# Five of nine key tiles of each head enter the value product as a rounded part and a rest

## The chip, the cores and the metric

The kernel runs on one core of a Trainium2 chip. The metric is the device time of one execution, in microseconds (us). The core's engines are named as the profile names them: PE (TensorE, matrix products; PEld is its loading of weights), DVE (VectorE), ACT (ScalarE), POOL (GpSimd) and SP (SyncE, whose queue issues all DMAs of this kernel). Each works through its own instructions in program order and waits for the others by semaphores.

## The reference

Three stages follow one another; all inputs and the output are float32.

```python
# attention: 2 batches x 8 heads, 1152 keys, 576 queries after pooling, width 64
q_pool = q.reshape(B, H, S // 2, 2, D).mean(axis=3)
scores = (1 / sqrt(D)) * (q_pool @ k.T)
attn = exp(scores - max(scores));  attn = attn / (sum(attn) + 1e-9)
x = attn @ v                                  # -> 1152 tokens x 512
# gated layer, 512 -> 1536 -> 512
x = ((x @ w_a) * (x @ w_b)) @ w_out
# four experts, 512 -> 1024 -> 512
p = probs / (probs.sum(-1) + 1e-9)
out = sum over e of p[:, e] * (max(x @ w1[e], 0) @ w2[e])
```

## The kernel before

**Attention.** The 16 heads go one after the other, and two heads (a pair) share their loads and preparations. Keys are cut into nine tiles of 128, queries into two halves of 288 columns (`HQ`). A score step `qk` (line 515) makes four products of a rounded format (fp32r): the high parts of keys and queries (L528, operands `A`, `QH`), then the rests together with the row of subtracted maxima (L533, `B`, `QL`). They fill one of two score buffers `st` in PSUM; ACT takes the exponential of 128x576 scores into a tile `e` in SBUF (L538), from a pool of `NE` = 8. A step `pv` (line 540) multiplies an `e` tile with the value tile `VF` in full float32 (L543): two products of 288 columns, and the profile has two records for each. `VF` holds the 64 value columns of the head, and ones in the other 64, so the same product gives the sum of the exponentials.

**The maxima.** For each pair, 27 max steps (`mx`) make a 128x384 product (L418) into one of two PSUM buffers, and DVE reduces it (L433). PE can thus be two max steps ahead of DVE. After the 27th, DVE folds the maxima into a column tile `mc` (L447), PE turns it by a product (L456), DVE copies the row (L458, `mr`), and a DMA puts it into `QL` of the next head; without it that head's scores can't start.

**Preparations of a pair** are `k` (the rounding of the keys, ACT), `klo0` to `klo2` (the rests of the keys in thirds of 128x384, DVE, L333), `qs`, `qh`, `ql` (the same for the queries) and the puts `da`, `db`, `dh`, `dl` (DMAs that lay them out as the operands of one head), `qb` (the operand `QB` of the max steps) and `row`. The loads are `lq`, `lk0` to `lk2` and `ldf` (values). `evac` copies a finished head out of PSUM (ACT), `nr`, `nb` and `n` divide it by its sums and split the result into `X`, high part and rest (L597, L283, L602).

**The order** of all of it is written out by hand: `FIRST` for heads 0 and 1, `PROG` for the rest, whose first nine lines that begin with `qk` are an even head and whose other nine are an odd one. A word stands for one step; a step goes to each engine's queue at the place where its word stands. In head 0, `A` and `C` are score steps on the first 256 and the last 320 queries, `x` and `y` the max steps of heads 0 and 1, `a` and `c` products with the values. The table `ENG` says which engine does a preparation (V is DVE, P is POOL, A is ACT).

**The later stages** (line 876 on) are products of three rounded terms (`mm3`, L884): high times high, high times rest, rest times high. While attention runs, the words `w` decode the first weights on DVE, ACT and POOL; POOL's only part in it is one subtraction per piece (L188). The first gated columns are started at the end of attention, and their products with the last pair come last.

Of the kernel before, what the change touches and what calls it, by code (L numbers as in the profile page):

```python
# [7 lines left out]
F32 = mybir.dt.float32  # L8
# [10 lines left out]
HQ = SQ // 2  # L19
# [28 lines left out]
C  # L48
C klo0 y a y a y c y c klo2 y y qh
C c y  # L50
# [17 lines left out]
qk n mx dl db mx pv pv da klo0 mx  # L68
qk mx pv
qk mx pv evac mx  # L70
qk lq klo1
qk mx mx pv mx pv ql mx ldf mx pv mx
qk klo2 lk0 mx
qk mx nr pv mx mx nb pv
qk w
qk mx dl lk1 mx pv qs mx dh
qk mx lk2 pv da w mx
qk mx db pv n mx n
qk pv mx evac k mx
qk w qh  # L80
qk qb n pv rm pv ldf
qk pv n pv w
qk
qk w n pv w
# [7 lines left out]
def kernel(  # L92
# [138 lines left out]

    with tc.manual_schedule():
        att = ExitStack()
        kq_p = att.enter_context(tc.tile_pool(name="kq", bufs=2))
        pair_p = att.enter_context(tc.tile_pool(name="pair", bufs=2))
        lo_p = att.enter_context(tc.tile_pool(name="lo", bufs=2))
        b_p = att.enter_context(tc.tile_pool(name="b", bufs=1))
        e_p = att.enter_context(tc.tile_pool(name="e", bufs=NE))
        m_p = att.enter_context(tc.tile_pool(name="m", bufs=2))
        u_p = att.enter_context(tc.tile_pool(name="u", bufs=2))  # L240
        r_p = att.enter_context(tc.tile_pool(name="r", bufs=1))
# [7 lines left out]
        def psum(kind, base, n, count):  # L249
# [5 lines left out]
        At, Bt, QHt, QLt, VFt = (  # L255
            [b_p.tile([128] + shape, dt, name=f"{n}{i}") for i in range(2)]
            for n, shape, dt in (
                ("A", [S], F32R), ("B", [S], F32R), ("QH", [SQ], F32R), ("QL", [SQ], F32R),
                ("VF", [KT, 128], F32),
            )  # L260
        )

# [9 lines left out]

        def fill_v(i, e):
            e.memset(VFt[i][:, :, rows(1 - i)], 1.0)

        engs = {"V": nc.vector, "P": nc.gpsimd, "A": nc.scalar}

# [11 lines left out]
        emitted = set()  # L289
        every = slice(0, 128)  # L290

        q_p = att.enter_context(tc.tile_pool(name="q", bufs=2))
        q_t = {}

        def load_first():
# [224 lines left out]
            if c == 1:  # L520
                den_gather(0, 0, U_t[0][64:65])

        def qk(h, t):
# [13 lines left out]
            e = E_t[h, t] = e_p.tile([128, 2, C1], F32, tag="e", name="e")[:, :, :HQ]  # L537
# [121 lines left out]
        nc.scalar.activation(out=nid, in_=nid_s, func=AF.Copy)  # L659
        own_qh(0, nc.scalar, c1)  # L660
# [8 lines left out]
        emitted |= {("row", 0), ("vf", 0), ("vf", 1)}  # L669
        emitted |= {(x, h) for x in "abhl" for h in range(2)}  # L670
        puts = {x: 2 for x in "abhl"}
        nxt_ld = {"lq": 2, "lk0": 2, "lk1": 2, "lk2": 2, "ldf": 2}
        nxt_pre = {"k": 1, "qs": 1, "qh": 1, "qb": 1}
        emitted |= {(x, 1) for x in ("lq", "lk0", "lk1", "lk2")} | {("ql", 0)}
# [13 lines left out]
        def first(tok):  # L688
# [22 lines left out]
            elif tok == "y":  # L711
                assert n < 5 * KR and {"dh1", "da1"} <= emitted
                max_step(1, n)
            elif tok == "R1":
                assert count["y"] == 5 * KR
                max_col(0, slice(5, 9))
                max_col(0, slice(9, 10), KR, 64)
                row_one()
                emitted.add(("row", 1))
            elif tok in ("E1", "E2"):  # L720
                assert count["ac"[tok == "E2"]] == KT
                evac_half(tok == "E2")
                emitted.add(("evac", 0) if tok == "E2" else "E1")
            else:
                need = {"kl1": "kh1", "ql1": "qh1", "dh1": "qh1", "db1": "kh1", "da1": "kl1"}
                assert tok not in need or need[tok] in emitted
                {
                    "qs1": lambda: own_qs(1, nc.gpsimd),
                    "qh1": lambda: own_qh(1, nc.scalar),
                    "kh1": lambda: own_kh(1, slice(0, S)),  # L730
                    "kl1": lambda: [own_klo(1, r, nc.gpsimd) for r in range(KR)],
                    "ql1": lambda: own_ql(1, nc.gpsimd),
                    "da1": lambda: own_put_kl(1, slice(0, S)),
                    "dh1": lambda: own_put_qh(1),
                    "db1": lambda: put(Bt[1][rows(1), :], At[1][rows(1), :]),
                    "lv1": lambda: [fill_v(1, nc.gpsimd), load_v(1)],
                    "zq": lambda: nc.gpsimd.memset(QB.bitcast(F32), 0.0),
                }[tok]()
                emitted.add(tok)

        for h in range(1, min(NHX, NH)):
# [3 lines left out]
            for tok in FIRST if h == 1 else PROG[half:] if h % 2 else PROG[:half]:  # L745
# [28 lines left out]
                elif tok == "pv":  # L774
# [3 lines left out]
                    assert ("qk", hh, j) in emitted  # L778
                    if j == 0:
                        assert ("vf", hh) in emitted  # L780
                    pv(hh, j)
                    pv_at[0] += 1
                elif tok == "evac":
                    fresh = 1
                    if h > 0:
# [20 lines left out]
                elif tok in ("lq", "lk0", "lk1", "lk2"):  # L806
                    p = nxt_ld[tok]
                    if p < NH // 2:
                        nxt_ld[tok] += 1
                        if tok == "lq":  # L810
                            assert ("qs", p - 1) in emitted
                            load_q(p)
                        else:
                            r = int(tok[2])
                            assert all((f"klo{x}", p - 1) in emitted for x in range(KR if r == 0 else r + 1))
# [46 lines left out]
            return  # L862

        rest = list(range(pv_at[0] - (NH - 1) * KT, KT))
        for j in rest:
            pv(NH - 1, j)
        evac(NH - 1)
# [197 lines left out]
```

## Time and profile before

| what | us |
| --- | --- |
| median of 3 runs | 907.93 (907.48 to 909.01) |
| the profiled execution, own time | 909.75 |
| its span, first to last instruction | 908.0 |
| busy: PE, DVE, ACT, POOL | 893.5, 459.1, 270.8, 72.1 |
| a pair of heads in the steady part (182.60 to 214.48) | 31.88 |
| end of attention, start of the gated layer's unbroken stretch | 282.4, 308.2 |

The granted TensorE clock is 1.00 in every stretch that the profile lists, which is the upper of its two levels, 2.4 GHz. Attention ends at 282.4 us, the other two stages take the rest. A busy time is the time in which an engine had an instruction running; ends of matmuls are modelled, so the spacing of their starts says more than their length. The chain of waits goes back from the last instruction, at each step to what released it.

### The profile page before, as it was taken

The numbers are of one execution on the slowest core, as the hardware profiler recorded it, in microseconds if no ns is written. First come the engines' busy times: TensorE is split into PE (matmuls) and PEld (weight loads), VectorE is DVE, ScalarE is ACT, GpSimd is POOL, SyncE is SP. The second block draws the span as 40 slices with busy tenths as digits, with TensorE's granted clock in tenths as the row PEclk, the third lists the DMA queues.
The fourth block names the chain that finished last, engine by engine and source line by source line (L and its number), as shares of the span: only waits on it lengthen the run. The fifth ranks groups of instructions, "written<-read, shape, count | busy, mean of one in ns | idle before, by whom it ended". The sixth has DMA issues, their size and how long they took to land.

```text
span 908.0 us, 11502 instructions
## 1 busy us (share of the span) xinstructions
PE 893.5 (98%) x4709; PEld 816.6 (90%) x4709; DVE 459.1 (51%) x792; ACT 270.8 (30%) x395; POOL 72.1 (8%) x43
## 2 busy tenths in 40 slices
PE   7999999999999999999999999999999999999998
PEld 5787888888889999999999999889988998899986
DVE  5875757766604888988785243113321242124311
ACT  4344455445453333333321232002300231003200
POOL 7000000000000222222222000000000000000000
PEclk9999999999999999999999999999999999999999
DMA  7557576857450222112222112001300121011011
GB/s 180 125 147 206 144 177 171 190 135 174 108 123 1 93 93 93 75 55 75 99 70 94 43 57 88 1 0 47 132 8 1 47 93 47 1 40 54 4 54 47
DMA packets 49385, 76.99 MB, mean 85 GB/s; under 512 B 32496, under 2 KB 36084, under 8 KB 45748
## 3 DMA queue, kind: packets, MB, share of 16 engines
q1 hardware_dynamic: 49332, 76.25, 29.5%
q8 instruction: 37, 0.61, 0.3%
q14 instruction: 16, 0.13, 0.0%
HBM read 51.96 MB, written 2.39 MB: 60 GB/s over the span
## 4 chain that ended last, share of the span: by engine, by line
PE 91%; DMA 3%; DVE 3%; ACT 1%; SPq 1%; issue 1%; ACTq 0%; DVEq 0%
PE PS L884 44%; PE PS L1007 22%; PE PS L543 12%; PE PS L418 4%; PE PS L528 3%; PE PS L533 3%; PE PS L508 1%; DMA kq<-in_kq_dram 1%; DMA dc<-D 1%; DMA B<-kh 1%; DMA QH<-QH 1%; DMA A<-kh 0%; DVE R L872 0%; SPq L390 0%; DMA rd<-rc 0%
## 5 line engine op out<-in xcount | busy, mean ns | idle before, releaser
L884 PE MATMUL PS<-X,w 128*128 128x384 f32 x2016 | 351.7, 335 | 0.6 <-ACT asb L910 0.5
L884 PEld LDWEIGHTS PS<-X,w 128*128 128x128 f32 x2016 | 349.8, 188 | 1.8 <-ACT asb L910 1.2
L1007 PE MATMUL PS<-w,hs 128*128 128x512 f32 x864 | 197.3, 390 | 0.0
L1007 PEld LDWEIGHTS PS<-w,hs 128*128 128x128 f32 x864 | 162.2, 188 | 33.3
L543 PE MATMUL PS<-e,VF 128*128 128x288 f32 x540 | 149.7, 408 | 0.7 <-ACT U L564 0.3
L433 DVE TENSOR_REDUCE m<-PS 128x1 f32<-128x384 f32 (+1 forms) x213 | 112.1, 554 | 57.9 <-PE PS L418 54.5
L980 ACT ACTIVATE hs<-PS 128x1152 fp32r<-128x1152 f32 x32 | 36.3, 1134 | 281.3 <-PE PS L884 281.3
L538 ACT ACTIVATE e<-PS 128x576 f32<-128x576 f32 x135 | 84.4, 648 | 108.0 <-PE PS L533 107.2
L543 PEld LDWEIGHTS PS<-e,VF 128*128 128x128 f32 x540 | 98.4, 190 | 20.0 <-ACT U L564 0.9
L981 DVE SCALAR_TENSOR_TENSOR hs<-PS,hs 128x1152 fp32r<-128x1152 f32 x32 | 43.5, 1358 | 134.3 <-ACT hs L980 134.3
L188 POOL TENSOR_TENSOR t<-v,w 128x512 f32<-128x512 f32 (+2 forms) x22 | 56.1, 2550 | 409.1 <-ACT w L178 367.9
L1016 DVE SCALAR_TENSOR_TENSOR acc<-PS,p_n,acc 128x512 f32<-128x512 f32 x27 | 20.3, 751 | 115.7 <-PE PS L1007 115.7
L884 PE MATMUL PS<-G,w 128*128 128x384 f32 x432 | 75.0, 334 | 0.0
L884 PEld LDWEIGHTS PS<-G,w 128*128 128x128 f32 x432 | 74.9, 188 | 0.0
L418 PE MATMUL PS<-kh,QB 128*128 128x384 f32 x189 | 72.7, 425 | 1.5 <-DVE m L433 1.1
L528 PE MATMUL PS<-QH,A 128*128 128x288 f32 x270 | 65.1, 322 | 2.6 <-ACT e L538 2.6
L533 PE MATMUL PS<-QL,B 128*128 128x288 f32 x270 | 57.4, 294 | 0.0
L528 PEld LDWEIGHTS PS<-QH,A 128*128 128x128 f32 x270 | 47.9, 189 | 9.0 <-ACT e L538 3.7
L418 PEld LDWEIGHTS PS<-kh,QB 128*128 128x128 f32 x189 | 34.9, 189 | 10.0 <-DVE m L433 4.2
L533 PEld LDWEIGHTS PS<-QL,B 128*128 128x128 f32 x270 | 43.3, 188 | 0.0
L223 DVE TENSOR_TENSOR w<-stg,w 128x1024 fp32r<-128x1024 f32 x32 | 38.9, 1215 | 8.1 <-ACT w L222 8.1
L193 DVE TENSOR_TENSOR w<-t,c 128x512 fp32r<-128x512 f32 (+2 forms) x44 | 39.2, 931 | 1.0
(84 smaller groups left out, 480.5 us busy)
## 6 DMA issues: line engine op xcount, KB each, us to landing
stg<-in_w_dram SPq DMA_DIRECT2D x16, 1024.0 KB
stg<-in_wab_dram SPq DMA_DIRECT2D x12, 1024.0 KB
stg<-in_wout_dram SPq DMA_DIRECT2D x8, 768.0 KB
VF<-in_vo_dram SPq DMA_DIRECT2D x16, 288.0 KB
A<-kl SPq DMA_DIRECT2D x15, 288.0 KB
q<-in_kq_dram SPq DMA_DIRECT2D x7, 576.0 KB
kq<-in_kq_dram SPq DMA_DIRECT2D x21, 192.0 KB
A<-kh SPq DMA_DIRECT2D x14, 288.0 KB
```

The lines of the kernel that those rows point to most:

```text
L188: nc.gpsimd.tensor_tensor(out=t, in0=v, in1=h.bitcast(F32), op=ALU.subtract)
L193: nc.vector.tensor_tensor(out=l, in0=t, in1=c, op=ALU.add)
L223: nc.vector.tensor_tensor(out=t[:, 1, :n], in0=s, in1=t[:, 0, :n].bitcast(F32), op=ALU.subtract)
L418: nc.tensor.matmul(out=out[:lhs.shape[1]], lhsT=lhs, rhs=rhs, start=True, stop=True)
L433: nc.vector.tensor_reduce(out=max_slot(h, qi)[:, r:r + 1], in_=mx[:n_q(h, qi)], axis=AX.X, op=ALU.max)
L528: nc.tensor.matmul(out=st[:, c, :HQ], lhsT=At[i][:, ks], rhs=QHt[i][:, c * HQ:(c + 1) * HQ], start=True, stop=False,)
L533: nc.tensor.matmul(out=st[:, c, :HQ], lhsT=Bt[i][:, ks], rhs=QLt[i][:, c * HQ:(c + 1) * HQ], start=False, stop=True,)
L538: nc.scalar.activation(out=e, in_=st[:, :, :HQ], func=AF.Exp, scale=1.0 / 16.0)
L543: nc.tensor.matmul(out=PS[:, c, :HQ], lhsT=VFt[h % 2][:, t, :], rhs=e[:, c, :], start=(t == 0), stop=(t == KT - 1),)
L884: nc.tensor.matmul(out=ps[n], lhsT=wt(kc)[:, wi, w0:w0 + 128], rhs=src(kc)[:, xi, n * TOK:(n + 1) * TOK], start=(kc == first and i == 0), ...
L981: nc.vector.scalar_tensor_tensor(out=gv(hs[:, 1, :]), in0=ph[:, :, :TOK], scalar=0.0, in1=gv(hs[:, 0, :].bitcast(F32)), op0=ALU.max, op1=A ...
L1007: nc.tensor.matmul(out=po, lhsT=cur[f][:, hi, ts], rhs=wv[:, wi, cs], start=(f == 0 and i == 0), stop=(f == NFE - 1 and i == 2),)
```

## The change

In heads 2 to 15, the five key tiles with a number below `NS` = 5 enter the value product in two parts. `eh` is the `e` tile rounded to fp32r and `el` the rest (128x576 each); `VH` and `VL` are the same two parts of the first five value tiles. The product becomes `eh`·`VH` + `eh`·`VL` + `el`·`VH`, three fp32r products for each of the two halves. The other four tiles, and heads 0 and 1, keep the float32 product. Key tiles are visited in the order 0, 5, 1, 6, 2, 7, 3, 8, 4, so split and whole tiles alternate; the last one is split. The words `eh`, `el`, `vh` and `vl` are added, `PROG` is a new order, and `ENG` names an engine for each `eh` and `el` (`el06` is the rest of step 6 of an even head, `el16` that of an odd one).

Of the ten rests of a pair POOL makes eight and DVE two; of the ten roundings ACT makes six, POOL two and DVE two. `klo0` and `klo1` go from DVE to POOL, the high part of `X` goes from ACT to DVE. The pools `kq` and `q` of loaded keys and queries have one buffer instead of two, `e` six instead of eight; `eh` and `el` have three each. Head 0 begins with three score steps ahead of its max steps, and one sum of queries there goes from POOL to DVE.

```diff
-NE = 8
+NE = 6
 FIRST = """
-A kh1 x x
-A x qh1 kl1 x dh1 ql1 da1 x
-A x lv1 a x a
-A x x a a zq a r1 db1 qs a y y k
+A kh1
+A qh1 kl1 dh1 ql1 da1
+A x lv1 x x
+A x a x x a x a x x a zq a r1 db1 qs a y y k
 ...
+NS = 5
+ORDER = (0, 5, 1, 6, 2, 7, 3, 8, 4)
+NEH = 3
 PROG = """
-dh mx mx rw
+mx da el
 ...
-ENG = {"qs": "V", "qh": "A", "k": "A", "ql": "V", "klo0": "V", "klo1": "V", "klo2": "V", "mult": "V", "xhi": "A", "xlo": "V"}
+ENG = {'qs': 'V', 'qh': 'A', 'k': 'A', 'ql': 'V', 'klo0': 'P', 'klo1': 'P', 'klo2': 'V', 'mult': 'V', 'xhi': 'V', 'xlo': 'V', 'el06': 'P', 'el14': 'V', 'eh02': 'A', 'eh14': 'V', 'eh08': 'P', 'vl': 'V', 'el02': 'P', 'el10': 'P', 'eh18': 'P', 'el18': 'P', 'eh16': 'A', 'vh': 'A', 'el00': 'P', 'el12': 'P', 'el04': 'P', 'eh00': 'V', 'el16': 'V', 'eh06': 'A', 'el08': 'P', 'eh12': 'A', 'eh10': 'A', 'eh04': 'A'}
 ...
-        kq_p = att.enter_context(tc.tile_pool(name="kq", bufs=2))
+        kq_p = att.enter_context(tc.tile_pool(name="kq", bufs=1))
 ...
+        def v_high(h):
+            i = h % 2
+            cast(eng("vh", "A"), VHt[i][:, :, rows(i)], VFt[i][:, :NS, rows(i)])
 ...
+        def e_high():
+            h, j = x = parts["eh"].pop(0)
+            H_t[x] = eh_p.tile([128, 2, HQ], F32R, tag="eh", name="eh")
+            cast(eng(f"eh{h % 2}{j}", "A"), H_t[x], E_t[x])
+            parts["el"].append(x)
+
+        def e_low():
+            h, j = x = parts["el"].pop(0)
+            L_t[x] = eh_p.tile([128, 2, HQ], F32R, tag="el", name="el")
+            eng(f"el{h % 2}{j}", "P").tensor_tensor(
+                out=L_t[x], in0=E_t[x], in1=H_t[x].bitcast(F32), op=ALU.subtract
+            )
 ...
-        def pv(h, t):
-            e = E_t.pop((h, t))
+        def pv(h, j):
+            i = h % 2
+            t = ORDER[j]
+            e = E_t.pop((h, j))
+            if split(h, j):
+                eh, el = H_t.pop((h, j)), L_t.pop((h, j))
+                mm = [(VHt[i][:, t, :], eh), (VLt[i][:, t, :], eh), (VHt[i][:, t, :], el)]
+            else:
+                mm = [(VFt[i][:, t, :], e)]
             for c in range(2):
-                nc.tensor.matmul(
-                    out=PS[:, c, :HQ], lhsT=VFt[h % 2][:, t, :], rhs=e[:, c, :],
-                    start=(t == 0), stop=(t == KT - 1),
-                )
+                for k, (lhs, rhs) in enumerate(mm):
+                    nc.tensor.matmul(
+                        out=PS[:, c, :HQ], lhsT=lhs, rhs=rhs[:, c, :],
+                        start=(j == 0 and k == 0), stop=(j == KT - 1 and k == len(mm) - 1),
+                    )
 ...
-        own_qs(0, nc.gpsimd, c1)
 ...
+        own_qs(0, nc.vector, c1)
```

The following three places show the order of the instructions, in a pair of the steady part. First PE, in an even head, from one reduction-fed max product to the next (L418, L437): before, a value product is one row of two float32 matmuls.

```order
L418 MATMUL PS_108<-kh_1575,QB_109 128x384 x2
L543 MATMUL PS_108<-e_1656,VF0_118 128x288 x2
L418 MATMUL PS_108<-kh_1575,QB_109 128x384
L543 MATMUL PS_108<-e_1662,VF0_118 128x288 x2
L418 MATMUL PS_108<-kh_1575,QB_109 128x384 x2
```

And now, a split tile, a whole one and another max product:

```order
L437 MATMUL PS_111<-kh_1531,QB_112 128x384
L592 MATMUL PS_111<-eh_1662,VH0_123 128x288
L592 MATMUL PS_111<-eh_1662,VL0_125 128x288
L592 MATMUL PS_111<-el_1702,VH0_123 128x288
L592 MATMUL PS_111<-eh_1662,VH0_123 128x288
L592 MATMUL PS_111<-eh_1662,VL0_125 128x288
L592 MATMUL PS_111<-el_1702,VH0_123 128x288
L437 MATMUL PS_111<-kh_1531,QB_112 128x384 x2
L592 MATMUL PS_111<-e_1648,VF0_121 128x288 x2
L437 MATMUL PS_111<-kh_1531,QB_112 128x384
```

A split tile has six matmuls instead of two, and each half takes its `eh` twice and its `el` once.

Second DVE, from the start of an even head: the reductions of max products (L433, L452) and what stands between them. Before:

```order
L433 TENSOR_REDUCE m_1083<-PS_108 128x1 x4
L333 TENSOR_TENSOR kl_1112<-kq_900,kh_1007 128x384
L433 TENSOR_REDUCE m_1083<-PS_108 128x1 x4
L333 TENSOR_TENSOR kl_1112<-kq_900,kh_1007 128x384
L433 TENSOR_REDUCE m_1083<-PS_108 128x1 x3
```

And now:

```order
L452 TENSOR_REDUCE m_1629<-PS_111 128x1 x4
L304 CAST eh_1662<-e_1639 128x576
L452 TENSOR_REDUCE m_1629<-PS_111 128x1 x3
L290 TENSOR_TENSOR VL0_125<-VF0_121,VH0_123 128x5x64
L452 TENSOR_REDUCE m_1629<-PS_111 128x1 x7
L352 TENSOR_TENSOR kl_1664<-kq_1374,kh_1531 128x384
```

Two of the three key rests have left this place, a rounding of `e` and the rest of the values stand in it.

Third POOL. Before, a pair holds at most one instruction of it, such as this one of 128x256:

```order
L188 TENSOR_TENSOR t_1820<-v_1818,w_1358 128x256
```

Now it holds these twelve, of which the first two serve the last tile of the pair before:

```order
L304 CAST eh_1608<-e_1603 128x576
L577 TENSOR_TENSOR el_1633<-e_1603,eh_1608 128x576
L352 TENSOR_TENSOR kl_1664<-kq_1374,kh_1531 128x384
L577 TENSOR_TENSOR el_1702<-e_1639,eh_1662 128x576
L577 TENSOR_TENSOR el_1733<-e_1658,eh_1694 128x576
L352 TENSOR_TENSOR kl_1664<-kq_1374,kh_1531 128x384
L577 TENSOR_TENSOR el_1781<-e_1700,eh_1729 128x576
L577 TENSOR_TENSOR el_1803<-e_1761,eh_1795 128x576
L304 CAST eh_1826<-e_1777 128x576
L577 TENSOR_TENSOR el_1864<-e_1777,eh_1826 128x576
L577 TENSOR_TENSOR el_1877<-e_1801,eh_1833 128x576
L577 TENSOR_TENSOR el_1904<-e_1822,eh_1888 128x576
```

Eight rests, two roundings and two key rests are POOL's, each with its inputs in SBUF.

## Rows read from the trace of the kernel before

**Rows 1.** The page's chain of waits, by line, shares of the span
```profile
PE PS L884 44%; PE PS L1007 22%; PE PS L543 12%; PE PS L418 4%; PE PS L528 3%; PE PS L533 3%; PE PS L508 1%; DMA kq<-in_kq_dram 1%; DMA dc<-D 1%; DMA B<-kh 1%; DMA QH<-QH 1%; DMA A<-kh 0%; DVE R L872 0%; SPq L390 0%; DMA rd<-rc 0%
```

**Rows 2.** Busy time by stretch: length, engines, PEclk, DMA share, GB/s
```profile
40.00:118.83 78.83, 75.46 (x395) 63.09 (x394) 53.52 (x118) 36.08 (x60) 0.73 (x1) 1.00 0.68 172
182.60:214.48 31.88, 31.88 (x173) 27.88 (x173) 22.50 (x52) 17.02 (x31) 0.74 (x1) 1.00 0.65 159
246.37:284.00 37.63, 36.95 (x192) 31.27 (x191) 3.05 (x7) 17.30 (x29) 0.00 (x0) 1.00 0.36 87
```

**Rows 3.** Chain of waits in a steady pair: start us, us, what
```profile
200.47 0.97 PE PS L543 x4
201.44 0.35 PE PS L418 x2
...
202.76 0.27 PE PS L528 x2
203.03 0.26 PE PS L533 x2
```

**Rows 4.** Groups by shape: busy us, mean ns of one, idle before
```profile
L433 DVE TENSOR_REDUCE m<-PS 128x1 f32<-128x384 f32 x207 | 109.0, 554 | 56.5 <-PE PS L418 53.1
...
L528 PEld LDWEIGHTS PS<-QH,A 128*128 128x128 f32 x270 | 47.9, 189 | 9.0 <-ACT e L538 3.7
...
L333 DVE TENSOR_TENSOR kl<-kq,kh 128x384 fp32r<-128x384 f32 x21 | 11.5, 549 | 0.0
...
L157 DVE TENSOR_SCALAR c<-c 128x512 f32<-128x512 f32 x20 | 7.7, 422 | 0.2
...
L340 DVE TENSOR_TENSOR qs<-q 128x576 f32<-128x576 f32 x7 | 5.3, 754 | 0.0
...
L283 ACT ACTIVATE qh<-qs 128x576 fp32r<-128x576 f32 x7 | 4.7, 676 | 0.0
```

**Rows 5.** POOL's instructions in order of time: start us, us
```profile
18.36 1.42 POOL L366 TENSOR_TENSOR QL<-qs,QH 64x576 fp32r<-64x576 f32 x1
19.84 0.58 POOL L274 MEMSET VF<- 128x576 f32 x1
...
186.79 0.74 POOL L188 TENSOR_TENSOR t<-v,w 128x256 f32<-128x256 f32 x1 [36.45 <-ACT w L178]
...
440.98 2.18 POOL L188 TENSOR_TENSOR t<-v,w 128x384 f32<-128x384 f32 x1 [10.31 <-ACT w L178]
```

**Rows 6.** DVE's instructions beside the last two of these
```profile
186.77 1.02 DVE L433 TENSOR_REDUCE m<-PS 128x1 f32<-128x384 f32 x2 [1.46 <-PE PS L418]
...
441.73 0.55 DVE L192 TENSOR_TENSOR t<-v,w 128x384 f32<-128x384 f32 x1
442.31 1.72 DVE L193 TENSOR_TENSOR w<-t,c 128x384 fp32r<-128x384 f32 x2
```

**Rows 7.** Waits from 40 to 118.8: us in total, times, longest
```profile
PE PS L528 <- ACT e L538: 2.6, 2, 1.8
```

**Rows 8.** Chain of waits at the start: start us, us, what
```profile
9.94 4.63 DMA QH<-QH
14.61 1.01 PE PS L418 x2
15.62 0.21 PE PS L498
...
23.83 0.35 PE PS L418 x2
```

**Rows 9.** SP's issue of the put that head 1's max steps need
```profile
18.44 0.51 SPq L390 DMA_DIRECT2D A<-kl  x1
```

**Rows 10.** Chain of waits across the end of attention
```profile
277.52 4.86 PE PS L543 x20
...
308.23 249.90 PE PS L884 x1440
```

**Rows 11.** ACT's last exponentials of attention
```profile
277.10 1.19 ACT L538 ACTIVATE e<-PS 128x576 f32<-128x576 f32 x2 [1.83 <-PE PS L533]
```

More of the change, by code (lines that the diff above doesn't have):

```diff
@@ L238 @@
         e_p = att.enter_context(tc.tile_pool(name="e", bufs=NE))
+        eh_p = att.enter_context(tc.tile_pool(name="eh", bufs=NEH))
         m_p = att.enter_context(tc.tile_pool(name="m", bufs=2))
@@ L254 @@
         QB = b_p.tile([128, 9, 128], F32R, name="QB")
-        At, Bt, QHt, QLt, VFt = (
+        At, Bt, QHt, QLt, VFt, VHt, VLt = (
             [b_p.tile([128] + shape, dt, name=f"{n}{i}") for i in range(2)]
@@ L274, in fill_v, with fill_parts, v_low @@
             e.memset(VFt[i][:, :, rows(1 - i)], 1.0)
+        def fill_parts(i, e):
+            e.memset(VHt[i][:, :, rows(1 - i)].bitcast(F32), 1.0)
+            e.memset(VLt[i][:, :, rows(1 - i)].bitcast(F32), 0.0)
+        def v_high(h):
+            i = h % 2
+            cast(eng("vh", "A"), VHt[i][:, :, rows(i)], VFt[i][:, :NS, rows(i)])
+        def v_low(h):
+            i = h % 2
+            eng("vl", "V").tensor_tensor(
+                out=VLt[i][:, :, rows(i)], in0=VFt[i][:, :NS, rows(i)],
+                in1=VHt[i][:, :, rows(i)].bitcast(F32), op=ALU.subtract,
+            )
         engs = {"V": nc.vector, "P": nc.gpsimd, "A": nc.scalar}
@@ L290 @@
         every = slice(0, 128)
-        q_p = att.enter_context(tc.tile_pool(name="q", bufs=2))
+        q_p = att.enter_context(tc.tile_pool(name="q", bufs=1))
         q_t = {}
@@ L521, in evac_half, with qk @@
                 den_gather(0, 0, U_t[0][64:65])
-        def qk(h, t):
+        H_t, L_t = {}, {}
+        parts = {"eh": [], "el": []}
+        def qk(h, j):
             i = h % 2
+            t = ORDER[j]
             st = psum("st", 4, 2, 2)
@@ L536, in qk, with split @@
                 )
-            e = E_t[h, t] = e_p.tile([128, 2, C1], F32, tag="e", name="e")[:, :, :HQ]
+            e = E_t[h, j] = e_p.tile([128, 2, C1], F32, tag="e", name="e")[:, :, :HQ]
             nc.scalar.activation(out=e, in_=st[:, :, :HQ], func=AF.Exp, scale=1.0 / 16.0)
-        def pv(h, t):
-            e = E_t.pop((h, t))
-            for c in range(2):
-                nc.tensor.matmul(
-                    out=PS[:, c, :HQ], lhsT=VFt[h % 2][:, t, :], rhs=e[:, c, :],
-                    start=(t == 0), stop=(t == KT - 1),
-                )
+            if split(h, j):
+                parts["eh"].append((h, j))
+        def split(h, j):
+            return h > 1 and ORDER[j] < NS
+        def e_high():
[10 more added lines that the diff above has]
+        def pv(h, j):
+            i = h % 2
+            t = ORDER[j]
+            e = E_t.pop((h, j))
+            if split(h, j):
+                eh, el = H_t.pop((h, j)), L_t.pop((h, j))
+                mm = [(VHt[i][:, t, :], eh), (VLt[i][:, t, :], eh), (VHt[i][:, t, :], el)]
+            else:
+                mm = [(VFt[i][:, t, :], e)]
+            for c in range(2):
+                for k, (lhs, rhs) in enumerate(mm):
+                    nc.tensor.matmul(
+                        out=PS[:, c, :HQ], lhsT=lhs, rhs=rhs[:, c, :],
+                        start=(j == 0 and k == 0), stop=(j == KT - 1 and k == len(mm) - 1),
+                    )
         def evac(h):
@@ L671 @@
         puts = {x: 2 for x in "abhl"}
+        nxt_v = {"vh": 2, "vl": 2}
         nxt_ld = {"lq": 2, "lk0": 2, "lk1": 2, "lk2": 2, "ldf": 2}
@@ L736, in first @@
                     "lv1": lambda: [fill_v(1, nc.gpsimd), load_v(1)],
-                    "zq": lambda: nc.gpsimd.memset(QB.bitcast(F32), 0.0),
+                    "zq": lambda: [nc.gpsimd.memset(QB.bitcast(F32), 0.0)] + [fill_parts(i, nc.gpsimd) for i in range(2)],
                 }[tok]()
@@ L780 @@
                         assert ("vf", hh) in emitted
+                    if split(hh, j):
+                        while (hh, j) not in L_t:
+                            (e_high if (hh, j) not in H_t else e_low)()
+                        assert ("vl", hh) in emitted
                     pv(hh, j)
                     pv_at[0] += 1
+                elif tok in ("eh", "el"):
+                    if parts[tok]:
+                        (e_high if tok == "eh" else e_low)()
+                elif tok in ("vh", "vl"):
+                    g = nxt_v[tok]
+                    if g == h:
+                        assert ("vf", g) in emitted and pv_at[0] >= (g - 1) * KT
+                        nxt_v[tok] += 1
+                        if tok == "vl":
+                            assert nxt_v["vh"] > g
+                        (v_high if tok == "vh" else v_low)(g)
+                        emitted.add((tok, g))
                 elif tok == "evac":
@@ L810 @@
                         if tok == "lq":
-                            assert ("qs", p - 1) in emitted
+                            assert ("qs", p - 2) in emitted
                             load_q(p)
@@ L814 @@
                             r = int(tok[2])
-                            assert all((f"klo{x}", p - 1) in emitted for x in range(KR if r == 0 else r + 1))
+                            assert all((f"klo{x}", p - 2) in emitted for x in range(KR if r == 0 else r + 1))
                             load_k(p, r)
@@ L864 @@
         rest = list(range(pv_at[0] - (NH - 1) * KT, KT))
+        while parts["eh"] or parts["el"]:
+            (e_high if parts["eh"] else e_low)()
         for j in rest:
```

34 lines of the change are left out of this document (17 added, 17 removed).

## Prediction

> **What bounds the kernel now.** I read the chain of waits by line first [rows 1]: nearly all of it is PE, and attention's share is the scores, the max steps and, largest, the value products of L543 with 12%. The busy time by stretch comes next [rows 2]: in a steady pair PE is busy for all of the 31.88 us, DVE for 22.50, ACT for 17.02, POOL for 0.74. From 40 to 118.83 us PE lacks 3.4 us, and the last pair, without max steps, leaves DVE almost idle. So in attention a microsecond taken from PE is a microsecond gained, as long as DVE, now at 71%, and POOL, now at 2%, keep up with what they are given. The sum below is made against the profiled execution's own 909.75 us, of which 1.75 lie outside its span; the median of the runs is 907.93, so I carry the difference over to that.
>
> **The value products.** A whole tile (L543 x4) costs PE 0.97 us in the chain [rows 3]. A score step has four fp32r matmuls of 288 columns, 0.27 and 0.26 for two [rows 3], so 0.1325 each. A split tile has six such matmuls: 0.795. That is 0.175 less, and 5 tiles in 14 heads are 70: -12.25 us. Each of the six loads other weights than the one before, but so do L528 and L533 in turn; a load (PEld of L528) takes 189 ns [rows 4], longer than 132.5, and the score step runs at 132.5 all the same, so loads overlap. A steady pair would go from 31.88 to 30.13.
>
> **What the other engines get, per pair.** DVE loses two key rests of 0.55 (L333 in [rows 4]). It gets two rests of 128x576 at 0.75 (L340, the same shape with two inputs, [rows 4]), two roundings of 128x576, two rests of the values (320 elements, at most the 0.55 of L333) and two high parts of `X` (half a rounding). A rounding on DVE isn't in the trace: by the one-input L157, 0.42 for 512 elements, it is 0.47, by the two-input L340 0.75; I take 0.47, since it has one input. Together +2.7 to +3.9, so DVE is busy 25.2 to 26.4 of 30.1 us. ACT gets six roundings of 0.68 (L283, [rows 4]) and two of the values and gives up two halves: under +5 on 17.0, with 8 us left. POOL gets eight rests, two key rests and two roundings. Its 64x576 subtraction took 1.42, a 128x256 one 0.74 [rows 5], which scaled up by 576/256 gives 1.67; I take 1.42 and for the key rest two thirds of it. Its rounding lies between the memset's 0.58 and 1.42; I take 1.0. With the 0.74 of before that is 16 of 30 us.
>
> None of this is PE's, but PE waits for it. What hides it is the distance in PE's queue: five or six score steps stand between a tile's scores and its product, some 6 us, against 0.65 for the exponential, 0.7 for the rounding and 1.4 for the rest. Without that cover a late rest stops PE where it stands, with the next scores queued behind. The exponentials find a free `e` buffer, since a split tile gives its own back as soon as the rest is made. SP's first load of keys waits, with one buffer, for the key rests on POOL and DVE; behind it stand the values of the next head and the puts of the queries. These are needed some 6 us later, and a loaded put takes up to 4.63 [rows 8]: I count nothing, at worst 1 us a pair. The puts of the next head's keys now stand behind the sums of the finished head, still 7 us ahead of their use: the same.
>
> **Where POOL and DVE meet.** The trace shows this in two places. A POOL subtraction of 128x256 beside reductions from PSUM took 0.74, at 186.8 [rows 5, 6]. One of 128x384 beside DVE instructions with both inputs in SBUF took 2.18 at 441, instead of about 1.0 [rows 5]; and DVE's two L193, 0.55 each like the L192 ahead of them, took 1.72 [rows 6]. POOL ended at 443.16; with 1.0 of work it began when L192 ended (442.28), and the L193 lost the 0.7 that POOL still needed. So either waits for the other's whole instruction. In a pair, eleven stretches of DVE's work now begin with an instruction with two inputs in SBUF, or a rounding; POOL is busy half of the time; a wait costs half of 1.42. That is 11 x 0.5 x 0.7 = 3.9 us of delay for DVE in each pair, and takes it to about 29.7 of 30.1.
>
> The Trainium skill, SBUF — State Buffer, section "Who interferes with whom", has the rule for this: a VectorE instruction with two SBUF inputs and a GpSimd instruction that reads SBUF exclude each other for the whole instruction, whoever is second waits, while a reduction doesn't contend. By it the sum is the one with waits (901.4, or 916 if they add up), without it 895. The trace agrees with it in both rows, 0.74 beside reductions and 2.18 beside two inputs.
>
> How much of the delay reaches PE? Today DVE waits for PE before its reductions, 53.1 us in 207 of them (L433, [rows 4]), 0.26 for each, so it follows closely, and PE can go two max steps ahead. In most of the eleven places this lead takes the delay. In three it doesn't: at the start of an even head, where a rounding and the values' rest stand among reductions one max step behind PE; at the column of maxima, for which PE waits before the row product; and at the two rests of an odd head that DVE makes itself late in the pair. Three times 0.5 x 0.7 is 1.0 us a pair, and six pairs have max steps: +6.0. The bounds are 0 (all leads suffice) and 3.9 less the little slack, 3.5 a pair, +21.
>
> **The ends.** Head 0: PE waits from 11.55 to 14.61 for a put [rows 8], in front of it stands one score step, now three, and four such matmuls of 0.21 [rows 8] move ahead twice: 1.7 us. But head 1's max steps need a put that is issued at 18.44 [rows 9], and by the 4.63 of the other one it lands at 23.1; they start at 23.83 [rows 8]. So 0 to 1.7 can be had, and 0.7 by these rows. The sum of queries that moves to DVE stands behind its reductions and may bring its put 0.4 later: I take -0.5.
>
> The pairs from 40 to 118.83 lose 2.6 us where PE waits for an exponential that stands behind the rounding of keys that came late [rows 7]. The loads and that rounding are farther apart now: between 0 and -2.6, and since the same weight loads crowd the queues there I take -1.0.
>
> The end of attention: today five whole tiles (4.86 us) follow the last scores [rows 10], and the exponentials are done 0.77 us after these tiles begin [rows 10, 11]. Now three tiles follow, of 0.80, 0.97 and 0.80, and the last is rounded and subtracted by POOL: 0.77 + 1.0 + 1.42, then four matmuls, 0.53, is 3.7 against 2.57 of work. So +1.2 (0.7 to 1.9), in a chain that runs on to 308.23 [rows 10].
>
> Sum: -12.25 + 6.0 - 0.5 - 1.0 + 1.2 = -6.55. The profile's own time would be 903.2, and the median 901.4.
>
> **Rivals.** First, the leads suffice everywhere and nothing reaches PE: -12.55 or a little more, 895. For it: in the steady pair PE doesn't wait once today, and POOL is only half busy. Against it: DVE's 71% go to about 85% before any delay.
>
> Second, and on the other side, DVE becomes the bound: at 29.7 of 30.1 it takes little to tip it. From 2.1 us of stall in each of the six pairs nothing is left of the gain (12.55 / 6), and with 3.3 a pair (most of the 3.9) the sum is -12.25 + 19.8 - 0.5 + 1.2 = +8.2: 916. For it: DVE's reductions come one behind another, a delay in one makes the next late, and the two PSUM buffers then stop PE. Against it: POOL is idle for several microseconds late in the pair, while it waits for a rounding on ACT behind the copying out of the finished head, so that it meets DVE less than half of the time there.
>
> Third, the gain is eaten just so: 1.8 to 2.4 us of stall a pair, 906 to 909.7.
>
> Fourth, the change doesn't save PE time at all: if the weight loads didn't overlap between products of three kinds, six would cost 6 x 0.189 = 1.13 us a tile, 0.16 more than now, +11 us, and with the other terms 925. The score step speaks against it.
>
> **How the numbers follow.** Forecast (part of the gain is kept, 898 to 905.9): 0.42. Nothing reaches PE (892 to 898): 0.25. Eaten just so: 0.10. DVE the bound (910 to 920): 0.20. Weight loads: 0.03. Two runs of this kernel can be told apart by 0.2%, or 1.8 us. Faster by more than that are the first two, 0.67; within it the third, 0.10; slower the last two, 0.23. The range takes in nearly all of the fast side and half of the slow one: 892 to 914.
>
> **What would show it.** In the profile after: records of L592 for split tiles, and chain pieces of about 0.8 us for six; a steady pair of 30.1 to 31.9 us; POOL's L577 at 1.4 us where DVE reduces and up to twice that beside its subtractions; PE's waits for DVE's reductions (L452), which are zero in the steady part today, and for POOL's rests. The prediction is wrong if a pair is longer than 31.9, if six matmuls take more than 0.97, or if PE has no wait for DVE or POOL at all.

## The result

The changed kernel takes 921.62 us (median of 4 runs, 919.45 to 923.16), the kernel before 908.47 on the same chip (4 runs, 907.48 to 909.11): ratio 1.0142, interval 1.0119 to 1.0166. Forecast were 901.4 us, with 892 to 914 as the range. It is slower, by 13 us, and outside the range. Of all the runs below one, of e8 with 916.03 us, was slow, and the times and ratios leave it out.

The profiled run of after is the fastest of the four, 919.45 us with a span of 917.7, and is 9.7 us longer than the profiled one of before. These 9.7 us are in attention, and the later stages only start later (the gated layer's unbroken stretch at 317.93 us, for 308.23 in [rows 10]). After's chain by line answers to [rows 1]:

```profile
PE PS L952 44%; PE PS L1075 21%; PE PS L592 9%; PE PS L437 3%; PE PS L551 3%; PE PS L556 3%; DMA QB<-qh 3%; DMA A<-kl 1%; DMA QH<-qh 1%; ACT e L561 1%; DMA kq<-in_kq_dram 1%; SPq L409 1%; PE PS L527 1%; POOL kl L397 1%; ACT D L611 0%
```

The value products (L543 before, L592 now) fell from 12% to 9%. New on the chain is the put `QB<-qh` with 3%; all transfers together take 6% of it by the same page, 3% before. The chain within a pair of after shows what became of the terms of [rows 3] (start us, us, what):

```profile
195.65 0.18 PE PS L437
195.82 0.39 PE PS L551 x2
...
196.48 0.44 PE PS L437 x2
...
201.55 0.18 PE PS L437
201.72 0.80 PE PS L592 x6
```

A split tile, six matmuls, takes 0.80 us, as forecast (0.795), and it took 0.97 whole. But at some places, like those shown, L551 x2 takes 0.39 where L528 x2 took 0.27, and L437 x2 takes 0.44 for 0.35: PE pauses between steps there. At others they take what they took before (L551 x2 0.27 at 195.11).

Busy time by stretch answers to [rows 2] (length, then PE, PEld, DVE, ACT, POOL, the granted clock, DMA share, GB/s). The three stretches of after are from 40 us to the first product run of the third pair, a pair further on, and the last pair. The first ends later in its pair than that of [rows 2], so their lengths can't be compared:

```profile
40.00:128.68 88.68, 84.69 (x489) 73.37 (x490) 66.20 (x144) 48.69 (x83) 31.42 (x26) 1.00 0.72 170
162.67:196.92 34.25, 31.52 (x194) 28.34 (x193) 25.89 (x59) 19.27 (x34) 15.19 (x13) 1.00 0.75 174
252.91:291.57 38.66, 34.81 (x214) 30.90 (x213) 14.26 (x25) 20.28 (x35) 15.38 (x12) 1.00 0.43 103
```

DVE (25.9 of a pair), ACT (19.3) and POOL (15.2) got just the work forecast (25.2 to 26.4, under 22, 16). But the pair is 34.25 us long, 2.4 more than before, and PE, never idle there before, lacks 2.7. From one row product (L475, L456 before) to the next, after's last five pairs with max steps take 32.8, 32.7, 34.0, 34.6 and 33.0 us, those of before 33.9, 33.0 and three times 31.9. For what PE waits is in the list of PE's waits from 40 to 300 us (us in total, times, longest):

```profile
PE PS L437 <- DMA QB<-qh: 6.8, 5, 2.2
PE PS L592 <- ACT U L608: 2.4, 6, 0.4
PE PS L551 <- ACT e L561: 1.5, 3, 1.0
PE PS L437 <- DVE m L452: 1.4, 4, 0.6
PE PS L592 <- ACT U L606: 1.4, 1, 1.4
PE PS L592 <- POOL el L577: 1.0, 1, 1.0
PE PS L551 <- DMA QH<-qh: 0.3, 1, 0.3
PE PS L475 <- DVE mc L466: 0.2, 1, 0.2
```

These are 15.0 us in 22 waits; the same list of before adds up to 3.8 in 6. Only 2.6 us are waits for DVE or POOL, where the forecast had its 6.0. The largest is the put of the next pair's wide queries `QB`. One such place, in SP's issues, then in the chain:

```profile
183.16 0.50 SPq L620 DMA_DIRECT2D dc<-U  x1
183.71 0.59 SPq L409 DMA_DIRECT2D A<-kh  x1
184.34 0.59 SPq L409 DMA_DIRECT2D A<-kl  x1
185.04 0.77 SPq L409 DMA_DIRECT2D QL<-ql  x1
185.91 1.41 SPq L340 DMA_DIRECT2D VF<-in_vo_dram  x1
187.42 1.63 SPq L409 DMA_DIRECT2D QB<-qh  x2
```

```profile
182.48 0.66 ACT U L608
...
183.19 1.06 PE PS L592 x6
...
188.42 5.44 DMA QB<-qh
...
194.00 0.41 PE PS L437
```

The sums `dc` can go only when ACT has copied them, at 183.14. Five issues stand ahead of the two `QB` puts, of which the later takes 5.44 us to land under this load. The new order begins a pair with a max step, which stands 2.24 us for them (PE's wait that ends at 194.00, the longest of the five). The second item of the list is here too: the next head's first product follows the finished head's last with two max steps between, and waits for the copy, so its six matmuls take 1.06.

Head 0 is 2.70 us later at its last products (chain: L592 x12 at 56.84, L543 x12 at 54.14 before). SP's issues show why; they answer to [rows 9]:

```profile
11.60 0.34 SPq L331 DMA_DIRECT2D q<-in_kq_dram  x1
18.70 1.28 SPq L337 DMA_DIRECT2D kq<-in_kq_dram  x3
...
20.60 0.59 SPq L409 DMA_DIRECT2D A<-kl  x1
```

The second pair's keys have one buffer now. Their load waits for the last reader of the first pair's keys, and the queue behind it waits too; the put of head 1's key rests is issued at 20.60, not 18.44, and PE stands 2.22 us for it at 26.21.

### The profile page after: what moved, and what is told of

It reads as the page before. It is cut to its first block, busy times and chain, and to the rows that moved or that the text cites. A ratio compares the mean times of both kernels' runs of the same rounds, so it can differ in the third digit from the quotient of the medians.

```text
span 917.7 us, 11990 instructions
## 1 busy us (share of the span) xinstructions
PE 889.9 (97%) x4849; PEld 819.3 (89%) x4849; DVE 487.9 (53%) x837; ACT 293.3 (32%) x435; POOL 176.5 (19%) x130
## 4 chain that ended last, share of the span: by engine, by line
PE 84%; DMA 6%; ACT 3%; DVE 2%; issue 2%; SPq 1%; POOL 1%; ACTq 0%; DVEq 0%; POOLq 0%
PE PS L952 44%; PE PS L1075 21%; PE PS L592 9%; PE PS L437 3%; PE PS L551 3%; PE PS L556 3%; DMA QB<-qh 3%; DMA A<-kl 1%; DMA QH<-qh 1%; ACT e L561 1%; DMA kq<-in_kq_dram 1%; SPq L409 1%; PE PS L527 1%; POOL kl L397 1%; ACT D L611 0%
## 5 line engine op out<-in xcount | busy, mean ns | idle before, releaser
L452 DVE TENSOR_REDUCE m<-PS 128x1 f32<-128x384 f32 (+1 forms) x213 | 113.4, 554 | 59.8 <-PE PS L437 55.7
L577 POOL TENSOR_TENSOR el<-e,eh 128x576 fp32r<-128x576 f32 x56 | 81.5, 1455 | 91.4 <-ACT eh L302 31.9
L592 PE MATMUL PS<-e,VF 128*128 128x288 f32 x260 | 73.6, 407 | 0.0
L437 PE MATMUL PS<-kh,QB 128*128 128x384 f32 x189 | 63.9, 375 | 8.5 <-DMA QB<-qh 6.8
L551 PE MATMUL PS<-QH,A 128*128 128x288 f32 x270 | 62.5, 313 | 2.4 <-ACT e L561 1.5
L592 PEld LDWEIGHTS PS<-e,VF 128*128 128x128 f32 x260 | 46.7, 189 | 7.3
L551 PEld LDWEIGHTS PS<-QH,A 128*128 128x128 f32 x270 | 46.3, 188 | 7.7 <-ACT e L561 4.6
L592 PE MATMUL PS<-eh,VH 128*128 128x288 f32 x140 | 48.1, 343 | 3.7 <-ACT U L608 2.4
L437 PEld LDWEIGHTS PS<-kh,QB 128*128 128x128 f32 x189 | 34.0, 188 | 16.9 <-DVE m L452 6.8
```

What stands on the lines that cost most here:

```text
L437: nc.tensor.matmul(out=out[:lhs.shape[1]], lhsT=lhs, rhs=rhs, start=True, stop=True)
L452: nc.vector.tensor_reduce(out=max_slot(h, qi)[:, r:r + 1], in_=mx[:n_q(h, qi)], axis=AX.X, op=ALU.max)
L551: nc.tensor.matmul(out=st[:, c, :HQ], lhsT=At[i][:, ks], rhs=QHt[i][:, c * HQ:(c + 1) * HQ], start=True, stop=False,)
L577: eng(f"el{h % 2}{j}", "P").tensor_tensor(out=L_t[x], in0=E_t[x], in1=H_t[x].bitcast(F32), op=ALU.subtract)
L592: nc.tensor.matmul(out=PS[:, c, :HQ], lhsT=lhs, rhs=rhs[:, c, :], start=(j == 0 and k == 0), stop=(j == KT - 1 and k == len(mm) - 1),)
```

## The experiments

Theory 1: the loss is waits on SP's queue and on copies that the new order puts next to their reader. Theory 2: it is the load of DVE and POOL and their port. All are measured against the kernel before, next to it on the same chip (a ratio of 0.001 is 0.9 us).

| run | median us | ratio to before, interval |
|---|---|---|
| after | 921.62 | 1.0142, 1.0119 to 1.0166 |
| e1_whole | 925.65 | 1.0181, 1.0157 to 1.0205 |
| e2_qb_first | 918.26 | 1.0104, 1.0080 to 1.0129 |
| e3_pair1_loads | 919.32 | 1.0115, 1.0093 to 1.0136 |
| e4_pv_later | 922.17 | 1.0143, 1.0119 to 1.0167 |
| e5_qb_and_pv | 919.27 | 1.0112, 1.0093 to 1.0132 |
| e6_all_moved | 911.13 | 1.0033, 1.0016 to 1.0050 |
| e7_all_moved_whole | 917.19 | 1.0099, 1.0086 to 1.0113 |
| e8_more | 903.97 | 0.9943, 0.9920 to 0.9965 |
| e9_more_loads_together | 908.02 | 0.9991, 0.9970 to 1.0011 |
| e10_more_whole | 912.67 | 1.0043, 1.0025 to 1.0061 |
| e11_before_loads_apart | 909.86 | 1.0011, 0.9995 to 1.0027 |

**e1: the new order without the split.**

```diff
         def split(h, j):
-            return h > 1 and ORDER[j] < NS
+            return False
         def v_high(h):   # and v_low
-            i = h % 2
+            return
```

> The changed kernel with its order, its buffers and its loads as they are, but every key tile goes into PV whole (two float32 matmuls), and the casts and subtractions that make the parts are left out: all 56 pieces on GpSimd, their casts, and the parts of V. Theory 1 (the 13 us over before are waits on SyncE's queue and on copies that the new order puts next to their reader; the extra work of VectorE and GpSimd costs nothing): TensorE has 70 x 0.17 = 12 us more to do, hides some of the waits behind it (up to 5 of the 8 us of waits for the wide queries), and still has the others: 925 to 932 us. Theory 2 (the waits come of VectorE and GpSimd, which have more to do and meet at their port): with that work gone the order costs nothing, and the time is that of the kernel before, 908, to 912 us.

925.65: theory 2 falls. With the parts' work on DVE and POOL gone (two key rests a pair stay on POOL, the high part of `X` on DVE), the new order, with its buffers and loads, is 16.5 us slower than before (ratio 1.0181). The split as such is a gain, but of 3.5 us (1.0181 against 1.0142, by the intervals some 3 either way) where its rows say 12.25. The list of waits shows `QB` with 1.4 here, not 6.8: longer products cover the wait that the split lays bare.

**e2: the wide queries ahead in SP's queue.**

```diff
-qk dl ldf w qb
+qk qb dl ldf w
```

> The changed kernel, with one word of the plan moved: the two puts of the next pair's wide queries (QB) are issued ahead of the low part of the queries and of the load of values, not behind them. Theory 1: the gaps of 1.0 to 2.5 us before the first max step of five pairs (8 us in all) shrink to under 0.5 us each: 5 to 8 us less than the changed kernel, 914 to 917 us. Theory 2: the waits come of the engines' load, and the order of SyncE's queue changes nothing: 920 to 923 us.

918.26, some 3.4 us less than after, where 5 to 8 were expected. From 80 to 250 us the list has no wait for `QB` any more, and a new one beside ACT's copy:

```profile
PE PS L556 <- DMA QL<-mr: 2.5, 5, 0.6
```

The put of the row of maxima, with two issues between it and `QB` in the same queue, is now the last to land. So the queue was the cause, and part of the gain went to what stands behind. Ahead of 80 us another part went: from 40 to 290 us PE waits 2.9 us for DVE's reductions, where after has 1.4, for the reason that e4 shows.

**e3: the second pair's loads taken out of the prologue.**

```diff
         row_direct(0)
-        load_q(1)
-        for r in range(KR):
-            load_k(1, r)
...
-    "da1": lambda: own_put_kl(1, slice(0, S)),
+    "da1": lambda: [own_put_kl(1, slice(0, S)), load_q(1)] + [load_k(1, r) for r in range(KR)],
```

> The changed kernel, with the four loads of the second pair's queries and keys taken out of the prologue and issued behind the third step of head 0, where their one buffer is about to be free. Theory 1 (these loads stop SyncE's queue from 11.6 to 18.7 us, and the puts of head 1's keys with it): head 0's end comes 2.2 to 2.7 us sooner, and the time is 2 to 2.7 us less than the changed kernel's: 918.5 to 919.5 us when that takes 921.6. Theory 2 (head 0 is later because GpSimd and VectorE fill and subtract more there): 0 to 0.5 us less.

919.32, 2.3 less than after, as theory 1 had it, though the two intervals overlap too far to call it clear of noise. The trace shows the mechanism: head 0's last products start at 55.03, 1.8 us sooner, and the put is the next issue ahead of the loads:

```profile
18.02 0.46 SPq L409 DMA_DIRECT2D A<-kl  x1
18.58 0.54 SPq L331 DMA_DIRECT2D q<-in_kq_dram  x1
19.21 1.71 SPq L337 DMA_DIRECT2D kq<-in_kq_dram  x3
```

**e4: the next head's first product a score step later.**

```diff
-... evac qs mx eh qh mx pv k el da
-qk dl ldf w qb
+... evac qs mx eh qh mx k el da
+qk dl ldf w qb pv
```

> The changed kernel, with one word of the plan moved: the first product of the odd head of each pair stands behind the next score step, not two max steps behind the last product of the even head, whose sums it overwrites. Theory 1: the wait of 0.66 us for ScalarE's copy of the sums, six times (4 us), goes, the score step covers it; the product waits nowhere else: 3 to 4 us less than the changed kernel, 917.5 to 918.5 us. Theory 2: ScalarE is late because of its load, and the wait turns up at the next step: 0 to 1 us less.

922.17: nothing gained, which theory 1 had not said. The wait for the copy is gone from the list of 40 to 290 us, which begins

```profile
PE PS L437 <- DMA QB<-qh: 8.0, 5, 2.4
PE PS L437 <- DVE m L452: 4.7, 3, 3.9
```

`QB` has grown from 6.8 to 8.0: PE came earlier to a put that came no earlier. The waits for DVE's reductions have grown by more, from 1.4 to 4.7. The 3.9 are one wait in the second pair, ahead of 79.22: DVE, in its own order, stands for a gather of 2 KB of sums (`dc<-D`) that is 11.16 us on its way beside the weight loads, and the reductions stand behind it. Behind it the granted clock is 0.73 from 79.2 to 82 and 0.76 from 82 to 86, means of its two levels. The profiled runs of e2, e3 and e5 have this place too, with 2.5 us each; after has 0.6. e3 changes nothing between head 0 and it, so in the profiled runs a part of what these edits saved was lost at a place that none of them moves, and e4 alone doesn't settle what the copy was worth.

**e5: e2 and e4 together.** Its edits are those two.

> The changed kernel with both edits of e2 and e4: the puts of the wide queries ahead of the queries' low part and the load of values, and the odd head's first product behind the next score step. Theory 1 (in e4 the 3 us saved at ScalarE's copy were given back in the wait for the wide queries, 9.3 us there against 8.1 before, because SyncE's queue had not become earlier): with that wait gone the saving stays, about 3 us less than e2, 914 to 916 us; part of it may be lost to the row of maxima, for whose put e2 waits 0.5 us a pair. Rival (ScalarE is late by its load, and the wait turns up again somewhere on it): the time of e2, 918 us.

919.27, not under e2: what e4 saves is given back again, now to the row of maxima, 6.1 us against 2.5 in e2:

```profile
PE PS L556 <- DMA QL<-mr: 6.1, 5, 1.4
```

(Its profiled run took 915.32, the least of its six.) Theory 1 has to be put more exactly: `A`, `QL`, `QB`, the values and the row stand in one queue behind the finished head's sums, the next pair's first steps need all of them but the values, and PE waits for the last of these, whichever that is.

**e6: all of the named waits moved, and e7: the same with whole tiles.** Beside e3's edit and e4's:

```diff
-qk dl ldf w qb
-qk rm pv pv pv pv ...
+qk qb w pv
+qk rm dl ldf pv pv pv pv ...
...
-... klo1 klo2 lk0 ldf mx nr w
-qk n ql
-qk pv
+... klo1 klo2 lk0 ldf mx w
+qk n ql
+qk pv nr
...   # last pair: U copied, and the last tile rounded and subtracted, on DVE
-                nc.scalar.activation(out=U[rows(o)], in_=both[rows(o)], func=AF.Copy)
+                nc.vector.tensor_copy(U[rows(o)], both[rows(o)])
```

> The changed kernel with all the waits moved away that its trace and e2 to e4 name, and with no less work on any engine: the wide queries' puts first and the row of maxima ahead of the load of values (8 us of waits, and the 3 us for the row that e2 showed in their place), the odd head's first product a score step later (3), the second pair's loads behind the third step (2.3), the reciprocal of the second pair one step later, and in the last pair the copy of the sums and the last piece's parts on VectorE (2.5). Theory 1: 13 to 17 us less than the changed kernel, 904 to 909 us. Theory 2 (VectorE and GpSimd carry too much, the waits only change their place): not under 914 us.

> e6 with every key tile whole in PV, the parts' casts and subtractions left out, as in e1. Theory 1: with the waits gone the 70 split tiles are worth nearly what the PV rows say, 70 x 0.17 = 12 us: 9 to 12 us more than e6. Theory 2: the split tiles are worth the 4 us by which e1 exceeds the changed kernel, or less, since their pieces load VectorE and GpSimd: 1 to 5 us more than e6.

e6 takes 911.13, some 10 us less than after (10.5 by the medians, 9.9 by the ratios); 13 to 17 were expected, and 914 was theory 2's floor. In its trace `QB`, the row and ACT's copy are off the list from 40 to 290 us; single places are on it:

```profile
PE PS L475 <- DVE mc L466: 3.0, 1, 3.0
PE PS L437 <- DVE m L452: 2.2, 3, 1.5
PE PS L551 <- ACT e L561: 1.5, 3, 1.0
PE PS L551 <- DMA kq<-in_kq_dram: 1.2, 1, 1.2
```

The first two are in the second pair, where DVE waits for sums (`dc<-D`, 9.93 us on their way) and reciprocals (`R<-rd`, 5.51), beside two weight loads of 1 MB. The split is worth 6.0 us now (1.0099 against 1.0033): more than in e1, less than theory 1 had it. Waits that e7's longer products cover are a part of that: the list of 40 to 290 us comes to 9.3 us in e6 and to 4.1 in e7.

**e8: the rest of the waits, and e9, e10, e11 to tell its parts apart.** On top of e6:

```diff
+        load_q(1)                       # in the prologue again, only the keys later
-pv evac db mx                ... qk mx pv mx mx dh pv eh
+pv evac db dh mx             ... qk mx pv mx mx pv eh
-                    if h == 2 and s == 2:
-                        w_dma()
-                        w_dma()
+                    if (h, s) in ((2, 2), (3, 4)):
+                        w_dma()
-                nc.scalar.activation(out=U[rows(1)], ...)        # odd heads: before the next exp
+                late.append(lambda: nc.scalar.activation(out=U[rows(1)], ...))   # qk runs it behind its exp
...   # the last head's rests all on DVE
```

> e6 with what its trace still shows as waits: the second pair's queries loaded in the prologue again and only its keys behind the third step (1.2 us for the wide queries at 33 us), the two loads of 1 MB of weights a head apart instead of together at 60 us (the waits of 1.7 and 4.2 us at 75 and 88 us, behind sums and reciprocals that take 6 to 10 us to land), the odd head's queries put beside its keys (1.4 us at 176 us), the copy of an odd head's sums behind the next exponential instead of before it (0.4 us a pair, 0.6 in the last), and the last head's low parts on VectorE. Theory 1: 5 to 8 us less than e6, 903 to 906 us, under the kernel before. Rival (the loads and copies only crowd another place): 909 to 912 us.

> e8 with the two loads of 1 MB together at 60 us again, as in the kernels before and after. If they crowd the small transfers of the second pair, 3 to 5 us more than e8; if the small transfers are late for another reason, the same as e8.

> e8 with every key tile whole in PV, the parts' casts and subtractions left out, as in e1 and e7. Theory 1: with nearly no wait left in e8, the 70 split tiles are worth what the rows of PV say, 70 x 0.17 = 12 us, less what longer PV hides: 9 to 12 us more than e8, 913 to 916 us. Theory 2: the split is worth the 4 to 6 us seen in e1 and e7: 908 to 910 us.

> The kernel before with only the two loads of 1 MB a head apart, as in e8. If e8 is faster because of the split, this changes nothing or little, since no wait of the kernel before stands on a transfer at 60 to 90 us: 907.5 to 909 us. If e8's gain is that of the loads alone: 904 to 905 us.

e8 takes 903.97 us, ratio 0.9943 (0.9920 to 0.9965), as theory 1 had it: 5 us less than the kernel before, some 18 less than after, with the same arithmetic on nearly the same engines. All waits in its list, 40 to 275 us, come to 3.1, the longest is 1.0:

```profile
PE PS L594 <- DVE U L610: 1.0, 1, 1.0
PE PS L551 <- ACT e L561: 0.7, 3, 0.3
...
PE PS L437 <- DMA QB<-qh: 0.3, 1, 0.3
...
```

e10, the same with whole tiles, is 8.7 us slower than e8 by the medians, 9.1 by the ratios: the split is worth 3.5, 6.0 and 9.1 us in three orders with ever fewer waits (each by the intervals some 2 to 3 either way). A pair shows it without the rest. The row product (L475) stands once in each pair; in a calm pair of e8 and one of e10 the places are

```profile
113.17 0.22 PE L475 MATMUL PS<-nid,mc 128*9 128x128 f32 x1
144.11 0.23 PE L475 MATMUL PS<-nid,mc 128*9 128x128 f32 x1
```

```profile
115.16 0.23 PE L475 MATMUL PS<-nid,mc 128*9 128x128 f32 x1 [0.21 <-DVE mc L466]
147.75 0.22 PE L475 MATMUL PS<-nid,mc 128*9 128x128 f32 x1
```

30.94 us with ten split tiles (30.84 to 31.68 in e8's five pairs from 81 us on), 32.59 without (32.59 to 32.97 in e10's), so 1.65 for ten tiles, 1.47 on the mean of the five pairs, where the forecast had 0.175 each. But 32.59 is 0.7 more than the 31.88 of before, with the same products. That is the new order's own price, in pauses of 0.1 to 0.2 us between steps; no run took them apart.

e9 is 4.0 us slower than e8 by its median. The profiled runs differ by only 1.1 (spans 903.0 and 901.9), so its traces explain a part: 0.5 us of waiting for `QH`, 0.3 more at `kq`. That the loads crowd small transfers is likely and not settled. e11 is 909.86, no different from the kernel before, so e8's lead over it isn't had by moving the loads alone; and e10, e8's order without the split, is 3.9 us slower than the kernel before (1.0043).

## Why the prediction was wrong

- **The value products**, -12.25: right in mechanism, and in the size of a tile (0.80 for six; 1.47 to 1.65 us a pair between e8 and e10, 1.75 forecast). Of the 12.25 the most that a run showed in the time is 9.1. The rival by which weight loads don't overlap, whose 925 lies nearest to the time, is excluded: by it six would take 1.13.
- **The work of DVE, ACT and POOL**: right to within 1 us a pair. The rests on POOL took what was taken for them, 1.42 (after's groups by shape: busy, mean ns of one, idle before):

```profile
L577 POOL TENSOR_TENSOR el<-e,eh 128x576 fp32r<-128x576 f32 x56 | 81.5, 1455 | 91.4 <-ACT eh L302 31.9 <-PE PS L437 25.9 <-DVE eh L304 22.1
```

- **DVE's delays that reach PE**, +6.0 (0 to 21): too large, and so was the delay itself, 3.9 us a pair, which was to take DVE to 29.7. The 25.9 measured hold all delays. In that pair the rows show one, of some 0.9: the two L171 of the rows below, 0.41 us each in e1, took 1.72 beside a rest on POOL. PE waits 2.6 us for DVE and POOL from 40 to 300 us, of which 0.95 are for the very last rest on POOL. Where a pair grew, this wasn't the cause, and the rival "DVE becomes the bound", whose price of 916 is near the result (it leaves out the -1.0 of the late keys; 915 with it), gives the wrong reason: e1 takes the parts' work off DVE and POOL and is slower still.

```profile
184.12 1.72 DVE L171 SCALAR_TENSOR_TENSOR v<-c,v 128x256 uint32<-128x256 uint32 x2
```

```profile
183.78 1.43 POOL L577 TENSOR_TENSOR el<-e,eh 128x576 fp32r<-128x576 f32 x1 [2.85 <-ACT eh L302]
```

- **The step that failed** is the sentence on SP's queue: "I count nothing, at worst 1 us a pair", and of the next head's puts, "the same". I gave each put its own time from issue to use. But the words `evac`, `da`, `dl`, `ldf`, `qb` and `rm` now stand together, so eight transfers wait for one copy of the sums and then for one another, and a pair begins with a max step, which needs the sixth and seventh of them. It cost 6.8 us in the list for `QB`, and more behind it: moving only `QB` gave back 3.4 (e2), the row put in its place cost 2.5. All the moves together gave back some 10 us (e6) and some 18 (e8). The prediction's own sign of being wrong, a steady pair longer than 31.9, came true with 34.0, 34.6 and 33.0.
- **A term that was missing**: the next head's first product overwrites the sums that ACT still copies. The diff shows it (`evac`, two max steps, `pv`); I checked the new order for late rests and not for early products. 2.4 us over the pairs, and 1.4 in the last. Mended alone it gained nothing (e4), because PE then waits longer at the put, and in the second pair for DVE.
- **Head 0**, -0.5: it became +2.7. The single buffer of keys was in the working for the steady pairs only; in the prologue it holds SP's queue from 11.94 to 18.70. In e3, with the loads moved, its last products start 1.8 us sooner.
- **Late keys at 40 to 118.8**, -1.0: the two waits of [rows 7] are gone (after's 1.5 us for exponentials are all in the last pair), but from row product to row product the three pairs there take 94.5 us (56.61 to 151.12) for 94.8 (53.91 to 148.72): new waits and pauses took the place of this term and of nearly all of the split's 1.75 a pair.
- **The end of attention**, +1.2: there are 0.95 at the last rest on POOL, as forecast, but 1.39 at the copy of the last pair's first head and 1.5 at exponentials stand ahead of it.

As an estimate the list adds up like this: 15.0 us of waits for 3.8 are +11.2. The step after a wait takes 0.23 to 0.26 us longer than in flow (the max step at 194.00 0.41 for 0.18, the six products at 183.19 1.06 for 0.80); 16 more such places make some +3.9. Pauses without a wait are 0.7 a pair, if e10's order is a measure for after's, so +4.2 in six pairs. Head 0 gives +2.7, the split -12.25. Together about +9.7, and attention ended 9.2 later (291.57 against 277.52 + 4.86, [rows 10]). The median is 13.2 apart and the profiled runs 9.7: the other three runs of after have 1.1 to 3.7 us more, which no trace here explains.

## What to carry to other kernels

Where an order is rewritten, go through the queue that issues the transfers as one more engine: write down, for every wait in it, all that stands behind, and for each cluster of transfers the first reader and the time from the common release to it. A saving on the busy engine brings it sooner to each of these readers, so that a transfer that was hidden comes to light, and a wait that is removed alone comes back at the next transfer of the same cluster. Measure a new order and a new arithmetic apart (here e1, e7 and e10): the order, with its buffers and loads, cost 16 us at first, the arithmetic saved up to 9, and the one time of the changed kernel shows neither.

## What the runs showed of the hardware

A rounding on DVE of 128x288, input and output in SBUF, takes 0.31 us alone and 1.40 beside a subtraction on POOL; a multiplication with two inputs 0.45 alone, 1.32 beside it. DVE's and POOL's instructions in the last pair of after:

```profile
255.99 0.31 DVE L304 CAST X<-U 128x288 fp32r<-128x288 f32 x1
...
275.32 1.32 DVE L646 TENSOR_TENSOR U<-U,R 128x288 f32<-128x288 f32 x1 [0.30 <-DMA R<-rd]
276.67 1.40 DVE L304 CAST X<-U 128x288 fp32r<-128x288 f32 x1
...
280.19 0.45 DVE L646 TENSOR_TENSOR U<-U,R 128x288 f32<-128x288 f32 x1
```

```profile
274.60 3.31 POOL L577 TENSOR_TENSOR el<-e,eh 128x576 fp32r<-128x576 f32 x2
```

The prediction had counted the two-input instructions from a row, and the roundings as an assumption. The Trainium skill, SBUF — State Buffer, section "Who interferes with whom", lists copies and casts among the instructions that can take the pair of ports shared with GpSimd; the 1.40 for 0.31 agrees with it.

A put from SBUF to SBUF of 144 KB took 4.0 to 5.4 us in after's chain; beside the two weight loads of 1 MB one put of `QH` took 9.18 (chain of after):

```profile
66.69 9.18 DMA QH<-qh
...
121.64 4.00 DMA QB<-qh
```

After PE had stood for 2.46 us until 76.08 in e2, its granted clock over the next 3.3 us was 0.52, the lower of its two levels for nearly all of it; after 2.24 us until 194.00 in the kernel after it stayed at 1.00. So a wait can cost more than its length, and need not. The stretches (length, engines, granted clock, DMA share, GB/s), of e2 and of after:

```profile
76.00:79.30 3.30, 3.22 (x12) 3.22 (x13) 1.61 (x4) 1.26 (x3) 0.82 (x1) 0.52 0.83 206
```

```profile
194.00:198.00 4.00, 4.00 (x24) 3.56 (x25) 2.98 (x6) 2.19 (x4) 1.84 (x3) 1.00 0.62 187
```
